# The first expert's w1 scaled quarter by quarter, buffers of their own for the first two attention blocks, and another order of early loads

## The chip, the cores and the metric

One core of one Trainium2 chip runs the whole kernel as one program. The metric is the device time of one execution in microseconds (us), taken as the median of several runs.

## The reference

Chunked attention comes first. For 4 batches and 8 heads of 64, each chunk of 32 queries sees 56 keys (16 to the left, its own 32, 8 to the right) and 8 memory keys. Its output `x` (3072 tokens by 512) goes into a mixture of 8 experts whose weights `P` come from a gate through 8 rounds of row and column normalising:

```
a = softmax(scale * q_c @ [mem_k, k_ctx].T);  x_c = a @ [mem_v, v_ctx]
logits = x @ w_gate;  P = exp(logits - max)
8 times: P /= P.sum(1) ; P /= P.sum(0) ; P *= N / E
for e in range(8):  out += P[:, e:e+1] * (relu(x @ w1[e]) @ w2[e])
```

All of it is float32. w1[e] is 512 by 1024, w2[e] is 1024 by 512.

## The kernel before

**Products.** TensorE multiplies in float16. Each float32 operand is scaled by a power of two and split into a high and a low float16 part, and three products (`PASSES`) stand for one. `split` (L508) does this: ScalarE writes the high part (L513), VectorE the low part (L521). The scale is found first: `most` (L555, its instruction at L558) reduces the absolute maximum per partition, and `scales` (L434) brings the partitions together by a transposition on TensorE (`turned_max`, L488, at L494), a reduction of one row (L502), a rounding to a power of two (L450, L451), a product with ones that spreads the value (L481) and a reciprocal (L456, L457). From the second expert on, the products follow a seven-product block scheme (`hidden`, `output`, with `product` at L1598).

**Tiles.** Tokens come in 6 units of 512 (`NU`), a unit in 4 attention blocks of 128 tokens and in two halves `g` of 256. A unit's work for one expert is 4 quarters `fp` of the 1024 hidden features. A w1 quarter is 512 by 256 floats, loaded by `load` (L536) in two transfers with rows of 128 floats (L549); a w2 quarter is one transfer (L551). The first unit of the first expert is done plainly: `first_hidden` (tile `pp`, L2045) makes 2 feature halves times 2 k halves times 6 matmuls of 256 columns for each quarter and half, and `plain_output` (tile `yp`, L2126) 6 matmuls of 512 columns for each quarter and block of tokens.

**Attention block n.** `load_block` (L848 for q, L842 to L845 for k), `load_extra` (rows `kx` that neighbour the block and the memory keys, L782 to L790) and `load_values` (v in windows, one transfer for each chunk and parity, L921; memory values L890) fetch it. Then: transpositions `tq` (L1006) and `tk` (L1010), copies into `qT` and `kC` (L1014 to L1034, ScalarE), scores `sp` (L1069), maximum and difference (L1083, L1089, VectorE), exp (L1108), transposition `ta` (L1127), values `xp` (L1137), division (L1155 to L1157), transposition `xt` (L1178), copy into `xg` (L1184). `qT` and `kC` exist once, so block 1 waits for block 0's scores. The first half's scale of x comes from the maxima of v of blocks 0 and 1 (L974).

**Order.** Nothing is scheduled by the compiler: each step is a task with an engine, a modelled cost, a priority and its predecessors. `Plan.run` (L164) takes for each engine the task that can start first, ties by priority, and writes the instructions in that order; each engine then runs its list strictly in order. Transfers are tasks of SP (some of ScalarE) with a modelled share `dma` of the transfer engines. Where TensorE would be idle over 0.4 us in the attention stage, `pad` (L126) fills in matmuls on the identity matrix whose result nobody reads (tile `warm`, L427). `BLOCKS`, `VALUES` and `FIRST` (L732 to L734) hold the priorities of the early loads; the lowest is first. Here w1's four quarters come behind q, k and v of blocks 0 and 1.

**First expert's weights.** `fetch_first` loads four quarters, finds four maxima and one scale over all (`scale_w`), and only then `plain1` (w1) or `plain2` (w2) may split any quarter.

## Time and profile before

| | us |
|---|---|
| median of 3 runs | 1921.87 |
| lowest, highest | 1920.07, 1922.44 |
| the profiled execution's own time | 1919.81 |
| its span, first to last instruction | 1917.9 |

The page gives busy time for each engine; TensorE's includes the `warm` matmuls, and its granted clock is 1.00 over the span. A row of instructions gives its start, its length, engine, line, operation, the tile written and read, and how often it stands there in a row (x); what is in square brackets is the engine's idle time before it and what ended it. The suffix q (SPq) means the issuing queue of that engine.

### The profile page before, as it was taken

Reading aid. Unit: us, or ns where it says so; the run is one execution under the profiler, and the core shown is the slowest. Engines: PE = TensorE matmul, PEld = TensorE weight load, DVE = VectorE, ACT = ScalarE, POOL = GpSimd, SP = SyncE. Lnnn points to the kernel's source line nnn. Section 1 sums busy time; section 2 is a strip of 40 time slices with the busy share of each in tenths; the row PEclk is TensorE's granted clock in tenths of the full one; section 3 lists DMA queues with packets and bytes.
Section 4 is the critical chain, followed back from the end, with each engine's and each line's share of the span. In section 5 each row is a group of like instructions: output and inputs, shape, how many; then the busy total and the mean of one; then the engine's idle time right before and its main releaser. Section 6 shows DMA issues by size and latency. Waiting matters only on the chain.

```text
span 1917.9 us, 47295 instructions
## 1 busy us (share of the span) xinstructions
PE 1903.2 (99%) x19616; PEld 1641.0 (86%) x19616; DVE 1436.4 (75%) x2396; ACT 1033.6 (54%) x2019; POOL 524.4 (27%) x549
## 2 busy tenths in 40 slices
PE   9999999999999999999999999999999999999999
PEld 7777676688888888888888888888888888888888
DVE  6776569778679866898668875898678885786565
ACT  4765565556456545646445554655555554564453
POOL 1220001544224221432124231342124232332112
PEclk9999999999999999999999999999999999999999
DMA  8678753453235342265214533245313732322321
GB/s 198 174 194 209 171 172 116 129 204 125 83 110 172 127 148 85 78 197 185 92 63 149 197 105 127 78 160 176 138 45 105 242 122 94 100 83 84 127 83 67
DMA packets 246791, 254.82 MB, mean 133 GB/s; under 512 B 113264, under 2 KB 180272, under 8 KB 242224
## 3 DMA queue, kind: packets, MB, share of 16 engines
q1 hardware_dynamic: 244452, 251.21, 41.2%
q8 instruction: 153, 2.51, 0.6%
q10 hardware_dynamic: 2124, 0.59, 0.2%
q14 instruction: 62, 0.51, 0.1%
HBM read 187.84 MB, written 63.44 MB: 131 GB/s over the span
## 4 chain that ended last, share of the span: by engine, by line
PE 96%; DMA 2%; DVE 1%; ACT 0%; issue 0%; SPq 0%; ACTq 0%; DVEq 0%
PE px L1598 26%; PE yx L1598 23%; PE pz L1598 13%; PE yz L1598 11%; PE py L1598 6%; PE yp L2126 6%; PE yy L1598 6%; DMA q<-in_q_dram 1%; PE xp L1137 1%; PE sp L1069 1%; PE pp L2045 1%; PE tq L1006 1%; PE tk L1010 0%; PE ta L1127 0%; PE xt L1178 0%; DVE w L521 0%
## 5 line engine op out<-in xcount | busy, mean ns | idle before, releaser
L1598 PEld LDWEIGHTS <-w 128*128 128x128 f16 x7896 | 771.4, 98 | 91.9 <-issue 0.6
L1598 PEld LDWEIGHTS <-h 128*128 128x128 f16 x7056 | 690.4, 98 | 81.4 <-issue 1.5
L1598 PE MATMUL px<-x,w 128*128 128x256 f16 x4512 | 549.1, 273 | 0.0
L1931 POOL TENSOR_TENSOR acc<-acc,y 128x256 f32<-128x256 f32 x252 | 267.5, 1068 | 862.1 <-ACT y L1906 842.7
L1598 PE MATMUL yx<-w,h 128*128 128x256 f16 x4032 | 467.5, 273 | 1.3 <-DVE acc L1941 1.3
L1657 ACT ACTIVATE q<-px 128x256 f32<-128x256 f32 x376 | 142.8, 381 | 294.2 <-PE px L1598 289.5
L1598 PE MATMUL pz<-x,w 128*128 128x256 f16 x2256 | 278.2, 273 | 0.0
L1598 PE MATMUL yz<-w,h 128*128 128x256 f16 x2016 | 233.8, 273 | 0.0
L1826 DVE TENSOR_TENSOR h<-ss,h 128x1024 f16<-128x1024 f32 x160 | 215.0, 1346 | 4.0 <-ACT h L1802 3.5
L1777 ACT ACTIVATE h<-c 128x768 f16<-128x768 f32 x168 | 140.8, 838 | 106.4 <-DVE c L1667 106.4
L1802 ACT CAST h<-ss 128x1024 f16<-128x1024 f32 x168 | 174.1, 1039 | 20.4 <-DVE ss L1766 19.6
L1766 DVE SCALAR_TENSOR_TENSOR ss<-c,ss 128x256 f32<-128x256 f32 x336 | 168.3, 501 | 8.2
L1810 DVE SCALAR_TENSOR_TENSOR h<-c,h 128x768 f16<-128x768 f32 x168 | 165.3, 984 | 9.2 <-ACT h L1777 9.1
L1667 DVE SCALAR_TENSOR_TENSOR c<-px,q 128x256 f32<-128x256 f32 x188 | 78.0, 422 | 103.2 <-PE px L1598 94.9
L1906 ACT ACTIVATE y<-yx,pscale 128x256 f32<-128x256 f32 x168 | 79.4, 473 | 114.8 <-PE yx L1598 110.6
L1598 PE MATMUL py<-x,w 128*128 128x256 f16 x1128 | 139.2, 273 | 0.0
L2126 PE MATMUL yp<-w,h 128*128 128x512 f16 x576 | 132.0, 379 | 0.0
L1667 DVE SCALAR_TENSOR_TENSOR c<-py,q 128x256 f32<-128x256 f32 x188 | 78.5, 422 | 60.2 <-PE py L1598 56.7
L1766 DVE SCALAR_TENSOR_TENSOR ss<-c,h 128x512 f32<-128x512 f32 x168 | 120.8, 719 | 3.1 <-ACT h L1754 3.0
L1598 PE MATMUL yy<-w,h 128*128 128x256 f16 x1008 | 116.9, 273 | 0.0
L2126 PEld LDWEIGHTS <-h 128*128 128x128 f16 x576 | 56.0, 98 | 57.9
L513 ACT ACTIVATE w<-ws,sw 128x1024 f16<-128x1024 f32 (+1 forms) x64 | 69.3, 1089 | 65.5 <-POOL ws L602 65.5
(158 smaller groups left out, 1773.0 us busy)
## 6 DMA issues: line engine op xcount, KB each, us to landing
x<-xkeep SPq DMA_DIRECT2D x28, 1792.0 KB
akeep<-acc SPq DMA_DIRECT2D x168, 256.0 KB
acc<-akeep SPq DMA_DIRECT2D x168, 256.0 KB
w1f<-in_moe_w_dram SPq DMA_DIRECT2D x72, 256.0 KB
w2f<-in_moe_w_dram SPq DMA_DIRECT2D x32, 512.0 KB
w1fm<-in_moe_w_dram SPq DMA_DIRECT2D x56, 256.0 KB
w2fm<-in_moe_w_dram SPq DMA_DIRECT2D x28, 512.0 KB
xkeep<-x SPq DMA_DIRECT2D x6, 1792.0 KB
```

The costliest lines, as they stand in the source:

```text
L513: lambda: nc.scalar.activation(dst(0), src(), AF.Copy, scale=s),
L1598: nc.tensor.matmul(dst.t, a, b, start=(not more and n == 0), stop=(n == end), skip_group_check=more,)
L1657: lambda: nc.scalar.activation(t.t, src.t, AF.Copy, scale=DOWN),
L1667: lambda: nc.vector.scalar_tensor_tensor(c.t[:, o], src.t, DOWN, q.t, op0=ALU.mult, op1=ALU.add),
L1766: lambda: nc.vector.scalar_tensor_tensor(dst(), src(), 0.0, other(), op0=ALU.max, op1=op),
L1777: lambda: nc.scalar.activation(h.t[:, 0, 0:3], c.t, AF.Relu),
L1802: lambda: nc.scalar.copy(h.t[:, 0, 3:7], ss.t),
L1810: lambda: nc.vector.scalar_tensor_tensor(h.t[:, 1, 0:3].rearrange("p a n -> p (a n)"), c.t.rearrange("p a n -> p (a n)"), 0.0, h.t[:, 0, 0 ...
L1826: lambda: spare.tensor_tensor(h.t[:, 1, 3:7], ss.t, h.t[:, 0, 3:7], op=ALU.subtract),
L1906: (lambda: nc.scalar.activation(t.t, src.t, AF.Copy, scale=f))
L1931: lambda: nc.gpsimd.tensor_tensor(acc.t[:, cols], acc.t[:, cols], q.t, op=ALU.add),
L2126: nc.tensor.matmul(py.t, hf.t[:, hl, where[fh], o : o + P], room(fp, WIDE * wl + DM * fh, WIDE * wl + DM * (fh + 1)), start=(fp == 0 and i ...
```

## The change

1. Each w1 quarter of expert 0 has a scale of its own. `total` replaces `most`: a sum of absolute values per partition, on ScalarE with an accumulating output for five of the eight quarters (`SUMS`), on VectorE for three. `scale_first` adds over the partitions by one product with ones and makes the scale with four small VectorE operations. w2's quarters keep a common scale, multiplied for each quarter by the inverse of w1's.
2. Blocks 0 and 1 have `qT`, `kC` and the transposed weights `aT` apart (lent from tiles that are idle yet), take `kx` straight from PSUM, and their larger copy into `kC` is on VectorE.
3. Memory values of batch 0 are loaded once and spread by GpSimd; all v loads of blocks 0 and 1 move to SP's queue and wait for that; the `kx` loads of blocks 0 and 1 move to ScalarE's queue. Three high parts of the first expert's splits (one w1, two w2) move to GpSimd.
4. A w1 quarter is 256 neighbouring columns: one transfer with rows of 256 floats, for all experts. w2's rows are grouped to match.
5. An exp on one column right at the start takes the load of ScalarE's table. Early loads with a priority below -10 start strictly in turn, over all queues. The planner's model of transfers is another one, with smaller costs; `PACE` goes from 38.0 to 38.4.

```
-ISSUE = 0.5
+ISSUE = 0.45
+LANES = 8
...
+        turns = sorted((t for t in self.tasks if t.dma and t.prio < IN_TURN), key=lambda t: t.prio)
+        for a, b in zip(turns, turns[1:]):
+            a.behind = [b]
+            b.left += 1
...
-                at = max(at, dma - BEHIND)
-                t.start = at
-                clock[t.eng] = at + t.cost
-                dma = max(dma, at + t.cost / 2) + t.dma
-                t.end = max(dma, at + t.cost) + 2.6
+                if self.fill is None:
+                    at = max(at, dma - BEHIND)
+                t.start = max(at, lanes[0])
+                for _ in range(t.count):
+                    at = max(at, lanes.pop(0))
+                    work = t.dma / t.count
+                    if self.fill is None:
+                        work *= SHARE
+                    dma = max(dma, at + BEGIN) + work
+                    lanes.append(dma + AFTER)
+                    at += ISSUE
+                clock[t.eng] = at
+                t.end = dma + AFTER
...
+    first = misc.tile([P, 1], F32, name="first")
+    nc.scalar.activation(first, one, AF.Exp)
...
-    PACE = 38.0
+    PACE = 38.4
...
+    def scale_first(fp, t, prio):
+        c = slice(fp, fp + 1)
+        whole = bank("att", [P, 1], f"whole_{fp}")
...
+            lambda: nc.tensor.matmul(whole.t, ones, mxs[:, 0, 0, c], start=True, stop=True),
...
+            nc.vector.tensor_scalar_max(u, whole.t, 2.0**-100)
+            nc.vector.tensor_scalar(
+                u.bitcast(I32), u.bitcast(I32), 0x7F800000, None, op0=ALU.bitwise_and
+            )
+            nc.vector.tensor_scalar_mul(u, u, 2.0**-14)
+            nc.vector.reciprocal(sf[:, 0, c], u)
...
+        def spared():
+            nc.gpsimd.tensor_scalar(dst(0), src(), s, None, op0=ALU.mult)
...
-    w1v = w1.rearrange("e (kt p) (fh fp f) -> e fp p kt fh f", p=P, fh=2, fp=FP)
-    w2v = w2.rearrange("e (fh fp p) d -> e fp p fh d", fh=2, fp=FP)
+    w1v = w1.rearrange("e (kt p) (fp f) -> e fp p kt f", p=P, fp=FP)
+    w2v = w2.rearrange("e (fp fh p) d -> e fp p fh d", fh=2, fp=FP)
...
-                for fh in range(2):
-                    queue.dma_start(st.t[:, fh], w1v[e, fp, :, :, fh])
+                queue.dma_start(st.t.rearrange("p k a f -> p k (a f)"), w1v[e, fp])
...
+            nc.scalar.activation(room(0, 0, 1024), st.t.rearrange(flat), AF.Abs, accum_out=dst)
...
-            sw[:, 0, 0:1],
-            [known[0, 1], ld],
+            sf[:, 0, fp : fp + 1],
+            [known[0, 1, fp], ld],
...
-    BLOCKS = (-50.0, -44.0, -30.0, -26.0)
-    VALUES = (-47.0, -41.0, -28.0, -24.0)
-    FIRST = (-38.0, -20.0)
+    BLOCKS = (-57.56, -49.14, -31.37, -14.83)
+    SUMS = ("AAAD", "ADAD")
+    KX_AT = -47.74
+    VALUES = (-45.76, -42.53, -25.94, -11.5)
+    FIRST = ((-46.33, -38.4, -19.16, -28.68), (-18.82, -23.03, -25.93, -18.46))
...
+                lv = [spread_out[n]]
             lv = lv + [
-                add(eng, parts, lambda i=i, on=on: go_v((i,), on), lv, at, [vt], dma=1.35)
-                for i, (eng, on) in enumerate(
-                    (("SP", nc.sync), ("ACT", nc.scalar) if n < 2 else ("SP", nc.sync))
-                )
+                add("SP", parts, lambda i=i: go_v((i,), nc.sync), lv, at + i, [vt], dma=VWORK)
+                for i in range(2)
             ]
...
-        kC = rings["kC"].take(lambda k: kC_tile)
+        if n == 1:
+            lent = operands("h", [P, 2, 7, GT], "early_operands", 3)
...
+            kC = rings["kC"].take(lambda k: piece(0, c=CB), 1)
+            qT = rings["qT"].take(lambda k: piece(HP * CB * KW), 1)
...
+        eng, copy = ("DVE", nc.vector.tensor_copy) if n < 2 else ("ACT", nc.scalar.copy)
...
-                dma=7.0,
+                dma=4.3,
...
+    t = add("ACT", 2, memory_rows, (), -49.4, dma=0.1)
+    spread_out.append(add("POOL", 0.9, lambda: spread(nc.gpsimd, 0), [t], -48.0))
+    spread_out.append(add("POOL", 1.1, lambda: spread(nc.gpsimd, 1), [t], -47.0))
```

## Rows read from the trace of the kernel before

**Rows 1.** The page: busy time of the engines over the span.

```profile
PE 1903.2 (99%) x19616; PEld 1641.0 (86%) x19616; DVE 1436.4 (75%) x2396; ACT 1033.6 (54%) x2019; POOL 524.4 (27%) x549
```

**Rows 2.** Busy time by stage: stretch, length, PE, PEld, DVE, ACT, POOL, PEclk, DMA share, GB/s.

```profile
0.00:34.00 34.00, 30.04 (x470) 24.40 (x471) 17.36 (x36) 14.71 (x26) 4.95 (x12) 1.00 0.82 182
34.00:66.00 32.00, 30.88 (x602) 23.38 (x602) 28.67 (x47) 24.07 (x46) 5.33 (x5) 1.00 0.74 173
66.00:120.00 54.00, 51.83 (x958) 38.90 (x959) 37.07 (x68) 37.51 (x77) 16.21 (x21) 1.00 0.77 207
120.00:290.00 170.00, 167.07 (x2982) 122.69 (x2960) 107.01 (x210) 96.19 (x198) 11.58 (x16) 1.00 0.69 181
```

**Rows 3.** The same view for line L427 (`warm`) alone: stretch, length, PE, PEld, PEclk.

```profile
0.00:34.00 34.00, 20.71 (x157) 15.83 (x157) 1.00 0.82 182
34.00:66.00 32.00, 0.49 (x3) 0.29 (x3) 1.00 0.74 173
```

**Rows 4.** Timeline from the last maximum of w1 to the first `pp` matmul.

```profile
26.36 1.21 DVE L558 TENSOR_REDUCE mxs<-w1f 128x1 f32<-128x1024 f32 x1
...
28.04 0.13 DVE L445 TENSOR_REDUCE most_of<-mxs 128x1 f32<-128x4 f32 x1
...
29.09 1.33 ACT L513 ACTIVATE x<-xg,sx 128x512 f16<-128x512 f32 x2 [0.42 <-DVE sx L457]
...
29.84 0.75 DVE L521 SCALAR_TENSOR_TENSOR x<-xg,sx,x 128x512 f16<-128x512 f32 x1 [0.32 <-ACT x L513]
...
30.70 0.16 DVE L457 RECIPROCAL sw<-uw 128x1 f32<-128x1 f32 x1
...
33.38 1.14 PE L2045 MATMUL pp<-x,w 128*128 128x256 f16 x6
```

**Rows 5.** Timeline of SP's queue, the early issues.

```profile
0.73 0.45 SPq L848 DMA_DIRECT2D q<-in_q_dram  x1
1.23 0.57 SPq L842 DMA_DIRECT2D k<-in_k_dram  x1
...
15.94 5.81 SPq L549 DMA_DIRECT2D w1f<-in_moe_w_dram  x8
...
24.08 5.50 SPq L921 DMA_DIRECT2D w<-in_v_dram  x8
...
30.79 4.06 SPq L921 DMA_DIRECT2D w<-in_v_dram  x8
```

**Rows 6.** Groups by line: VectorE and ScalarE to 66 us, GpSimd to 110 us.

```profile
L521 DVE SCALAR_TENSOR_TENSOR w<-w1f,sw,w 128x1024 f16<-128x1024 f32 x4 | 4.9, 1278 | 0.0
L558 DVE TENSOR_REDUCE mxs<-w1f 128x1 f32<-128x1024 f32 x4 | 4.8, 1212 | 0.0
...
L513 ACT ACTIVATE w<-w1f,sw 128x1024 f16<-128x1024 f32 x4 | 4.4, 1143 | 0.0
...
L1034 ACT ACT_TABLE_LOAD x1 | 1.3, 1283 | 9.1 <-DMA v_pair<-in_v_dram 9.1
...
L602 POOL TENSOR_TENSOR ws<-w1f 128x256 f32<-128x256 f32 x7 | 5.1, 726 | 33.4 <-DMA w1f<-in_moe_w_dram 16.8 <-DMA v_pair<-in_v_dram 7.3 <-ACT x L513 5.5
L602 POOL TENSOR_TENSOR ws<-ws,w1f 128x256 f32<-128x256 f32 x4 | 4.1, 1028 | 0.3
...
L913 POOL COPY w<-v_pair 128x1040 f32<-128x1040 f32 x2 | 2.1, 1050 | 11.5 <-DMA v_pair<-in_v_dram 11.5
```

**Rows 7.** The chain that ended last: its first DMA piece, and one run of 24 matmuls.

```profile
1.84 4.79 DMA k<-in_k_dram
...
402.74 2.62 PE yy L1598 x24
```

**Rows 8.** Timeline: the first `yp` matmuls.

```profile
55.87 1.46 PE L2126 MATMUL yp<-w,h 128*128 128x512 f16 x6
```

**Rows 9.** Waits of TensorE for data from 34 to 300 us: total, times, longest.

```profile
PE tq L1006 <- DMA q<-in_q_dram: 2.4, 3, 1.1
```

**Rows 10.** One five-us stretch, columns as in the view of rows 2.

```profile
20.00:25.00 5.00, 4.55 (x98) 3.63 (x96) 4.97 (x7) 1.80 (x3) 0.00 (x0) 1.00 1.08 302
```

More of the change, by code (lines that the diff above doesn't have):

```diff
@@ L23 @@
 HSHIFT = 18
-ISSUE = 0.5
+HFIRST = 12
+ISSUE = 0.45
+LANES = 8
+VWORK = 1.1
+WORK2 = 1.8
+BEFORE = 0.7
+TABLE = 0.9
+COLD = 4.5
 BEHIND = 5.0
-FIRST = 2.0
+SHARE = 1.5
+BEGIN = 1.0
+AFTER = 1.2
+LATER = 1.0
 MARGIN = 8.0
@@ L29 @@
 FAR = 60.0
+IN_TURN = -10.0
 class Task:
-    __slots__ = ("eng", "cost", "fn", "prio", "left", "ready", "end", "then", "takes", "frees", "n", "dma", "start", "many")
+    __slots__ = ("eng", "cost", "fn", "prio", "left", "ready", "end", "then", "takes", "frees", "n", "dma", "start", "many", "count", "behind")
 class Past:
@@ L110, in add @@
         t.many = many
+        t.behind = ()
+        t.count = cost
         if dma:
@@ L217, in run @@
                     heappush(self.free[b.group], (b.end, b.bank))
+            for s in t.behind:
+                s.left -= 1
+                s.ready = max(s.ready, t.start)
+                if s.left == 0:
+                    heappush(waiting[s.eng], (s.ready, s.n, s))
             lag = 0.0 if t.dma else 0.2 if t.eng == "PE" else 0.12
@@ L384, in tile_chunked_attn_sinkhorn_moe @@
     ring("at", range(1))
+    ring("aT", range(2))
     ring("g", range(3))
@@ L431, in tile_chunked_attn_sinkhorn_moe, with scales @@
     counted = [0]
-    def scales(part, s, u, name, deps, prio, pool=None):
+    def scales(part, s, u, name, deps, prio, pool=None, shift=SHIFT):
         n = s.shape[-1]
@@ L824, in load_extra @@
             return
-        t1 = part(slice(0, 2 * KR), loads[0:2], at, tx, tx)
+        t0, t1 = [
+            add(
+                "PE",
+                0.35,
+                lambda n=n: turn(slice(n * KR, (n + 1) * KR)),
+                loads[n : n + 1],
+                at + n,
+                [kx],
+                takes=None if n else tx,
+            )
+            for n in range(2)
+        ]
         t2 = part(slice(2 * KR, P), loads[2:4], needed(1) - 2.0, tx, None)
-        extra[u] = (kxT, [t1, t1, t2, t2])
+        extra[u] = (kxT, [t0, t1, t2, t2])
+        straight.append(tx)
+    straight = []
+    more = []
     def flat(t, i, r=slice(0, P)):
@@ L938, in load_values @@
             fill_ones = add("POOL", 0.3, lambda: nc.gpsimd.memset(vt.t[:, :, :, D:DV], 1.0), (), at, [vt])
-        parts = CB + (first or last)
+        parts = CB + (n == EARLY - 1)
         if n < BU:
@@ L1618, in hidden @@
         nm = f"{e}_{u}_{fp}"
+        down = DOWN if e > 0 else DOWN0
         (w, wmade), (x, xmade) = wo[e, fp, 1], xops[u]
@@ L1656, in read @@
                 0.4,
-                lambda: nc.scalar.activation(t.t, src.t, AF.Copy, scale=DOWN),
+                lambda: nc.scalar.activation(t.t, src.t, AF.Copy, scale=down),
                 [dep],
@@ L1706, in hidden @@
                 0.4,
-                lambda: nc.scalar.activation(c.t[:, 3], px.t, AF.Copy, scale=DOWN),
+                lambda: nc.scalar.activation(c.t[:, 3], px.t, AF.Copy, scale=down),
                 [t4],
@@ L1744, in hidden @@
             0.4,
-            lambda: nc.scalar.activation(rr(1), px.t, AF.Relu, scale=DOWN),
+            lambda: nc.scalar.activation(rr(1), px.t, AF.Relu, scale=down),
             [t4],
@@ L2171, in fetch_first @@
         for fp in range(FP):
-            st, ld = load(0, fp, which, FIRST[which - 1] + 0.5 * fp)
-            staged.append((st, ld))
-            found.append(most(0, fp, which, st, [ld], at - 12.0))
-        scale_w(0, which, found, at - 10.0, "att")
+            st, ld = load(
+                0, fp, which, FIRST[which - 1][fp], after=spread_out[:1] if which == 1 and fp else ()
+            )
+            if which == 1:
+                o = operands("w1", [P, 2, 7, 2, P], f"w1_0_{fp}")
+                staged.append((st, ld, o))
+            else:
+                staged.append((st, ld))
@@ new lines, in fetch_first, with together @@
+            found.append(total(0, fp, which, st, [ld], at - 12.0 + ((17.68, 19.5, 24.87, 5.01), (3.31, -26.43, 9.29, -16.2))[which - 1][fp]))
+            if which == 1:
+                found[-1].ready = SINCE[fp]
+            if which == 1:
+                c = slice(fp, fp + 1)
+                known[0, 1, fp] = scale_first(fp, found[-1], at - 10.0 + fp)
+        if which == 1:
+            known[0, 1] = known[0, 1, FP - 1]
+            return staged
+        def together():
+            nc.vector.tensor_tensor(mxs[:, 0, 1], mxs[:, 0, 1], uf, op=ALU.mult)
@@ L2232, in turn @@
                     plan.free[group] = []
-            att_tasks = lgs + [xkept[v] for v in range(KEEP)] + list(gkept.values())
+            att_tasks = lgs + [xkept[v] for v in range(KEEP)] + list(gkept.values()) + list(sxs.values())
             opened[0] = add("-", 0.0, turn, att_tasks, -2000.0)
```

278 lines of the change are left out of this document (181 added, 97 removed).

## The prediction

> **What bounds the kernel now.** I read the page first: TensorE is busy 1903.2 of 1917.9 us [rows 1], so only what makes TensorE idle, or busy with nothing, can cost or save time. The view by stages tells where that is [rows 2]: TensorE's idle time is the length less its busy time, 3.96 us before 34 us, 1.12 from there to 66, 2.17 to 120, 2.93 to 290. Then the same view for the `warm` filler alone [rows 3]: 20.71 us before 34 us and 0.49 to 66. So up to 34 us TensorE does 30.04 - 20.71 = 9.3 us of work that counts, and 24.7 us are waste; behind that the stages to 290 us lose 6.2 us of idle time and hardly any filler. The start is what can be won. All DMA, VectorE and ScalarE times matter only as far as they move the first `pp` matmul, at 33.38 [rows 4], or leave TensorE without work later.
>
> Read back from 33.38, two legs end together [rows 4]. The x leg: the first half's x is split from 29.09 on (its first low part starts at 29.84). The w1 leg: the last of four maxima ends at 27.57, the reduction over partitions starts at 28.04, the scale is there at 30.86, 2.8 us later, and only then a first quarter is split. Both lie behind one queue: SP issues w1's eight transfers from 15.94 to 21.75 [rows 5].
>
> **The w1 leg after the change.** Needed for the first `pp` is one quarter, 512 KB, in place of 2 MB. It stands seventh or so in turn, in front of v. At 302 GB/s, the rate of the stretch in which w1 comes [rows 10], 512 KB take 1.7 us. q, k of two blocks and kx are some 1.2 MB before it; at 200 GB/s (an estimate below that rate, since their rows are shorter) 6 us from about 2 us on. So it is there by about 11. Then a sum, 1.2 us on ScalarE: no such row, bounds 1.14 (an activation of the same size) and 1.14 + 1.28 (a table load, if Abs were to need one) [rows 6]; I take 1.2. One product and four small operations with their hand-overs: the old reduction had seven and took 2.8 [rows 4]; 1.5 for the new one. A split 1.14 + 1.28 [rows 6]. The quarter is ready at about 17; it no longer decides.
>
> **The x leg after the change.** It ends with block 1's v. SP issues first: four transfers for q and k, 0.45 to 0.57 each [rows 5], 2.0; two for kx, 1.1; one for w1, 5.81 / 8 = 0.73. That ends at 0.73 + 3.8 = 4.5. The v transfers now wait for the memory values, which ScalarE issues behind its table load of 1.28 [rows 6] and kx, so at about 3.5. Their landing has no row: a k transfer took 4.79 from its issue, with the first loads around it [rows 7], the upper end; no row excludes next to nothing for 16 KB, the lower; half of 4.79, 2.4, taken. Then GpSimd spreads them, 1.05 by its copy of 1040 columns [rows 6]: v starts at about 7.0. Sixteen issues follow on SP, at 4.06 / 8 = 0.51 to 5.50 / 8 = 0.69 each [rows 5]; at 0.55, nearer to the end with less in the queue, they end at 15.8. ScalarE's queue no longer shares this. Landing 2.4 again, maximum 1.2, scale 2.8 as for w1, split of x 0.67 + 0.75 [rows 4, 6]: **23.6 for the first `pp`**. The ends: 17.5, where the w1 leg takes over, if both landings take next to nothing and an issue 0.45; 30.6 if both take 4.8 and an issue 0.69. Block 1's own chain from v to `xg` (values, division, transposition, copy, some 3.8 us) runs beside the scale and ends earlier. That block 1 has buffers of its own takes its transpositions and scores out of block 0's way, and the larger copy of its keys off ScalarE; behind v's landing both are hidden, so I give them nothing. With v at its lower end the chain of 3.8 would be the next to decide, as long as the maximum and the scale together. ScalarE's queue gets five issues of kx and memory values ahead of its first copy; at 0.57 at most they end near 4.8, when the first k lands [rows 5, 7], and if they ended 1 us later block 0 alone would be later, which waits for v anyway.
>
> **What the start is worth.** Before the first `pp` TensorE did 9.3 less the 0.6 of `pp` before 34, 8.7 us, some of it for block 2, which will come later: 7.4 remain. Waste until the first `pp`: before 33.4 - 8.7 = 24.7, after 23.6 - 7.4 = 16.2. **Gain 8.5**, ends 14.6 and 1.5.
>
> **What is given back.** From 23.6 on TensorE needs work. There are 96 `pp` matmuls of the first half (4 quarters of 24), 2.62 / 24 = 0.109 each [rows 7], 10.5 us, and block 2, 3.7 us as half of the 7.4: 14 us. The outputs `yp`, at 55.87 before [rows 8], need all of w2. Behind v stand three quarters of w1, four of w2, q, k and v of block 2: 4.5 MB, 15 us at 302 GB/s, so about 33; a sum, a scale over all (2.8), a split: about 41. 17.4 us to fill with 14.2: 3.2 us of waste, where the old stage to 66 us lost 1.12 + 0.49 [rows 2, 3]. **Given back 2**, rounded up; ends 0, if block 3 comes in time to fill, and 6, if w2 comes 4 us later. VectorE is the other limit: 17.36 + 28.67 = 46 us of work up to 66 us [rows 2], of which five sums of 1.21 go to ScalarE [rows 6] and about 4 us come (two copies, four scales): 44 us, from 7 us on, so the whole of w2 is split at about 53 at the earliest; `yp` takes it quarter by quarter.
>
> Three high parts go from ScalarE to GpSimd. Its copy of about that size took 1.05; its additions with two inputs 0.73 for 256 columns, and 1.03 in another group of the same form [rows 6]. Ends 1.05 and four times 1.03; both hidden by the other quarters' `pp`, so nothing in the sum. The Trainium skill, GPSIMD Engine Reference, section Key points, speaks against this move: GpSimd shares its SBUF interfaces with VectorE and contends with VectorE instructions that read two SBUF inputs. VectorE's low parts are of that kind; the 0.73 and 1.03 would fit that, but no row proves it. By it each of the three would wait for a low part of 1.28, and the sum would be up to 1.3 us worse.
>
> **Later.** One w1 transfer for two saves SP issues beyond the start, the splits read w1 with a stride, and `PACE` moves by 0.4: TensorE does not wait there for weights, so nothing for all three; without that cover the issues would be 0.73 each. The new model of transfers reorders all of the stage to 290 us, whose 6.2 us of idle time [rows 2] could fall or grow: 0, ends -3 and +3. Behind it nothing changes but the start. Sum: 8.5 - 2 = 6.5. The profiled 1919.81 becomes 1913.3; it stands 2.06 under the median, so **1915.4** against 1921.87.
>
> **Rivals.** *Nothing to do* (0.17): loads of w1 and w2 come as late as the upper ends, TensorE waits between `pp` and `yp` what it waited before it. For it: 6 us given back, and 302 GB/s is a full rate already, with a DMA share of 1.08 [rows 10]. Against it: bytes moved before 34 us were only 182 GB/s on average [rows 2]. Gain 8.5 - 6 = 2.5, down to 0: 1919.4 to 1922. In the same case falls that a scale for each quarter does not do what it says because splits queue on VectorE in another order. *More* (0.13): the x leg near its lower end, later idle time falls too: gain 12 to 15, 1907 to 1910. *Slower* (0.12): attention of the blocks behind the start. The old model counted 7.0 for a store of x where the new one counts 4.3, and 1.55 for q where it is now 1.25, so loads are planned closer to their use, and TensorE, in order, stands at `tq` when q is late. It did so three times, 2.4 us in total, 1.1 at most [rows 9]. Twenty blocks come behind the first four. From 10 such waits of 1.1 the gain of 6.5 is gone and 3.8 us are lost beside, about 1926. Against it: only three of the blocks waited so far, and the new order loads earlier.
>
> **How the numbers follow.** The forecast has 0.58: its own range is 1911 to 1919. 0.2% of 1921.87 is 3.8 us, about what a measurement can tell from no change; faster is below 1918.0. Forecast 0.54 below it, and *more* 0.13, with 0.05 of *nothing to do* if little is given back: 0.72. Same: 0.04 and 0.12 of these, 0.16. Slower 0.12. The range takes the forecast, most of *nothing to do* and half of *more*: 1907 to 1922.
>
> **What would show it.** Right: first `pp` at 20 to 28 us; `warm` before 34 us at 8 to 14 in place of 20.7; SP's v issues from 7 to 17 without pause; `yp` from 40 to 46; waits at `tq` up to 300 us under 4 us in total. Wrong: a first `pp` behind 30, or TensorE idle or in `warm` for over 6 us between it and `yp`, or a total of waits at `tq` over 8.

## The result and the profile after

| | before | after |
|---|---|---|
| median, us (21 runs each, taken together) | 1920.89 | 1923.85 |
| the profiled execution's own time | 1919.81 | 1925.82 |
| its span | 1917.9 | 1923.9 |

The ratio is 1.0015, 95% interval 1.0009 to 1.0022: slower by 3 us, clear of the noise but inside the 0.2% that was named as no change, outside the range of 1907 to 1922, and on the other side of the forecast of 1915.4. The profiled execution of after is the second longest of its 21 and stands 1.97 above its median, that of before 1.08 below its own, so the spans differ by 6.0 where the medians differ by 2.96.

The page of after answers to [rows 1]: TensorE has 101 matmuls fewer, all fillers and more (58 `warm` in place of 168), and still a longer span.

```profile
PE 1898.3 (99%) x19515; PEld 1634.6 (85%) x19515; DVE 1436.9 (75%) x2407; ACT 1035.3 (54%) x2025; POOL 546.7 (28%) x555
```

The stages, as in [rows 2], with three finer stretches:

```profile
0.00:34.00 34.00, 27.85 (x483) 22.47 (x483) 20.04 (x46) 17.54 (x36) 11.09 (x16) 0.95 0.89 209
34.00:66.00 32.00, 28.97 (x574) 20.75 (x575) 26.86 (x52) 23.53 (x45) 11.73 (x7) 1.00 0.67 142
66.00:120.00 54.00, 45.14 (x797) 32.74 (x796) 33.51 (x58) 32.11 (x66) 17.04 (x21) 0.94 0.82 214
120.00:290.00 170.00, 168.47 (x3016) 125.91 (x3018) 108.72 (x209) 98.94 (x207) 12.37 (x16) 1.00 0.66 171
...
85.00:90.00 5.00, 0.48 (x3) 0.49 (x4) 1.71 (x2) 2.08 (x5) 1.43 (x3) 0.76 0.99 243
90.00:95.00 5.00, 5.00 (x85) 4.17 (x85) 1.06 (x3) 2.13 (x4) 1.39 (x3) 0.56 0.78 192
95.00:100.00 5.00, 5.00 (x93) 3.30 (x92) 2.57 (x6) 3.74 (x9) 0.00 (x0) 1.00 0.85 232
```

The same view for `warm` alone, as in [rows 3]:

```profile
0.00:34.00 34.00, 8.92 (x54) 5.96 (x54) 0.95 0.89 209
34.00:66.00 32.00, 0.60 (x4) 0.39 (x4) 1.00 0.67 142
```

These two views give a sum. Waste (idle time and `warm`) before 34 us is 34 - 27.85 + 8.92 = 15.07 in place of 24.67: 9.6 less. A mean granted clock of 0.95 over 34 us takes about 1.7 of that back (an estimate: 5% of the length). From 34 to 66 it is 3.63 in place of 1.61: 2.0 given back. So up to 66 us the change wins 5.9; 6.5 was forecast. Then comes the loss: from 66 to 120 us TensorE is idle for 8.86 in place of 2.17, and the clock of 0.94 costs 3.2 more: 9.9 lost. The stage to 290 wins 1.4. By this sum the change is 2.6 behind at 290 us.

The sum is too kind to the change, as a mark in both kernels shows: the first `yx` (the second expert's first output product) starts 5.0 later (before first, then after).

```profile
399.96 2.24 PE L1598 MATMUL yx<-w,h 128*128 128x256 f16 x19
405.00 2.24 PE L1743 MATMUL yx<-w,h 128*128 128x256 f16 x19
```

What the sum misses, 2.4 us, stays open; possibly TensorE counts as busy also where its matmuls stand loosely, and the 9.6 is too high; no run shows it. From there to the end some 1.2 more go (below).

Most of the loss has one place in this execution. TensorE's timeline of after and its waits from 34 to 300 us, against [rows 9]:

```profile
82.00 0.82 PE L2191 MATMUL pp<-w,w 128*128 128x256 f16 x6
89.52 0.90 PE L1135 MATMUL tq<-ident,q 128*128 128x128 f32 x3 [6.70 <-DMA q<-in_q_dram]
```

```profile
PE tq L1135 <- DMA q<-in_q_dram: 7.3, 2, 6.7
```

And SP's queue in front of it (after first, then before, with TensorE's two rows):

```profile
77.64 0.45 SPq L1401 DMA_DIRECT2D xkeep<-x  x1
78.18 0.39 SPq L622 DMA_DIRECT2D w1f<-in_moe_w_dram  x1
78.66 1.58 SPq L970 DMA_DIRECT2D q<-in_q_dram  x1
```

```profile
78.32 0.60 SPq L1256 DMA_DIRECT2D xkeep<-x  x1
79.01 0.45 SPq L848 DMA_DIRECT2D q<-in_q_dram  x1
...
87.14 0.86 PE L1137 MATMUL xp<-x_room,at 64*32 64x65 f32 x64
89.10 0.66 PE L1006 MATMUL tq<-ident,q 128*128 128x128 f32 x4 [1.10 <-DMA q<-in_q_dram]
```

The q of block 8 stands behind the first store of x (1792 KB) in both kernels and lands some 10 us after its issue in both: 78.66 to 89.5, and 79.01 to 89.1. Before, TensorE had `pp` and `xp` until 88, so only 1.1 us of it showed; that is the 1.1 of [rows 9]. After, TensorE's list has `tq` next at 82.8. Behind the wait the granted clock is 0.56 for five us, most of it at 1.2 GHz. The kernel's own plan says why: with the store at 4.3 it has q landing at 75.8 and `tq` at 77.4, while SP issues q 12.7 us later than planned (78.66 against 66.0). The plan of the kernel before, with the old model of transfers, has it landing at 88.3, close to what was measured (89.1).

Of the start, SP's queue (as in [rows 5]), the engines around the first `pp` (as in [rows 4]), the high parts on GpSimd (as in [rows 6]), and the first `yp` (as in [rows 8]):

```profile
7.04 0.39 SPq L622 DMA_DIRECT2D w1f<-in_moe_w_dram  x1
8.51 7.85 SPq L1038 DMA_DIRECT2D v_pair<-in_v_dram  x16
```

```profile
12.89 1.05 ACT L646 ACTIVATE w<-w1f 128x1024 f16<-128x1024 f32 x1
13.85 0.19 ACT L646 ACTIVATION_READ_ACCUMULATOR w<-w1f 128x1 f32 x1
...
19.36 1.22 DVE L1086 TENSOR_REDUCE vmax<-v_pair 128x1 f32<-128x1024 f32 x1 [1.80 <-DMA v_pair<-in_v_dram]
20.61 0.15 DVE L492 TENSOR_REDUCE most_of<-vmax 128x1 f32<-128x2 f32 x1
20.68 1.28 DVE L595 SCALAR_TENSOR_TENSOR w<-w1f,sf,w 128x1024 f16<-128x1024 f32 x1
...
22.84 0.69 DVE L1302 TENSOR_TENSOR xq<-xp,rec 128x512 f32<-128x512 f32 x1
...
23.63 0.16 DVE L504 RECIPROCAL sx<-ux 128x1 f32<-128x1 f32 x1
24.95 0.59 ACT L1329 COPY xg<-xt 128x512 f32<-128x512 f32 x1 [0.26 <-PE xt L1323]
25.57 1.34 ACT L587 ACTIVATE x<-xg,sx 128x512 f16<-128x512 f32 x2
25.83 1.20 DVE L649 TENSOR_REDUCE mxs<-w1f 128x1 f32<-128x1024 f32 x1
26.94 1.41 DVE L595 SCALAR_TENSOR_TENSOR x<-xg,sx,x 128x512 f16<-128x512 f32 x2
27.17 0.35 PE L542 MATMUL whole<-mxs,one 128*128 128x1 f32 x2
27.39 1.06 PE L2191 MATMUL pp<-x,w 128*128 128x256 f16 x6
```

```profile
L582 POOL TENSOR_SCALAR w<-w2f,sf 128x1024 f16<-128x1024 f32 x2 | 6.0, 2986 | 18.1 <-DVE most_of L492 11.3 <-PE xp L1282 6.8
...
L582 POOL TENSOR_SCALAR w<-w1f,sf 128x1024 f16<-128x1024 f32 x1 | 3.8, 3827 | 10.4 <-DMA w<-in_v_dram 10.4
```

```profile
47.84 1.46 PE L2272 MATMUL yp<-w,h 128*128 128x512 f16 x6
```

The first `pp` comes at 27.39 (before 33.38, forecast 23.6), the first `yp` at 47.84 (before 55.87, forecast 41).

### The profile page after: what moved, and what is told of

It is laid out like the page before. It is cut to its first block, busy times and chain, and to the rows that moved or that the text cites. A ratio compares the mean times of both kernels' runs of the same rounds, so it can differ in the third digit from the quotient of the medians.

```text
span 1923.9 us, 46983 instructions
## 1 busy us (share of the span) xinstructions
PE 1898.3 (99%) x19515; PEld 1634.6 (85%) x19515; DVE 1436.9 (75%) x2407; ACT 1035.3 (54%) x2025; POOL 546.7 (28%) x555
## 4 chain that ended last, share of the span: by engine, by line
PE 91%; DVE 4%; DMA 2%; SPq 1%; issue 1%; ACT 1%; POOL 0%; ACTq 0%; DVEq 0%; POOLq 0%
PE px L1743 24%; PE yx L1743 23%; PE pz L1743 12%; PE yz L1743 11%; PE py L1743 6%; PE yy L1743 6%; PE yp L2272 5%; PE xp L1282 1%; DMA q<-in_q_dram 1%; DVE ss L1912 1%; PE sp L1199 1%; DVE h L1956 1%; PE pp L2191 1%; PE xt L1323 1%; DVE x L595 1%
## 5 line engine op out<-in xcount | busy, mean ns | idle before, releaser
L2077 POOL TENSOR_TENSOR acc<-acc,y 128x256 f32<-128x256 f32 x252 | 276.9, 1106 | 865.5 <-ACT y L2052 852.3
L1972 DVE TENSOR_TENSOR h<-ss,h 128x1024 f16<-128x1024 f32 x160 | 207.0, 1296 | 3.7 <-ACT h L1948 3.7
L1948 ACT CAST h<-ss 128x1024 f16<-128x1024 f32 x168 | 174.2, 1040 | 25.2 <-DVE ss L1912 24.9
L1912 DVE SCALAR_TENSOR_TENSOR ss<-c,ss 128x256 f32<-128x256 f32 x336 | 172.7, 514 | 8.2
L1956 DVE SCALAR_TENSOR_TENSOR h<-c,h 128x768 f16<-128x768 f32 x168 | 166.1, 989 | 10.7 <-ACT h L1923 10.5
L1813 DVE SCALAR_TENSOR_TENSOR c<-pz,q 128x256 f32<-128x256 f32 x188 | 78.7, 422 | 26.7 <-PE pz L1743 25.4
```

The source lines that it names most:

```text
L1813: lambda: nc.vector.scalar_tensor_tensor(c.t[:, o], src.t, down, q.t, op0=ALU.mult, op1=ALU.add),
L1912: lambda: nc.vector.scalar_tensor_tensor(dst(), src(), 0.0, other(), op0=ALU.max, op1=op),
L1948: lambda: nc.scalar.copy(h.t[:, 0, 3:7], ss.t),
L1956: lambda: nc.vector.scalar_tensor_tensor(h.t[:, 1, 0:3].rearrange("p a n -> p (a n)"), c.t.rearrange("p a n -> p (a n)"), 0.0, h.t[:, 0, 0 ...
L1972: lambda: spare.tensor_tensor(h.t[:, 1, 3:7], ss.t, h.t[:, 0, 3:7], op=ALU.subtract),
L2077: lambda: nc.gpsimd.tensor_tensor(acc.t[:, cols], acc.t[:, cols], q.t, op=ALU.add),
```

## The experiments

Eighteen kernels. An interval reaches about 0.001 to either side of its ratio, 2 us, so the profiles, one execution of each kernel, carry much of the argument. "First pp" and "first yx" are the starts of these matmuls; "waits" are TensorE's at `tq`, `tk` and `tx` for q, k and kx from 34 to 300 us, total. Before has 33.4, 2.4 and 400.0.

| run | built on | first pp | waits | first yx | ratio to before, interval |
|---|---|---|---|---|---|
| after | | 27.4 | 7.5 | 405.0 | 1.0015 (1.0009 to 1.0022) |
| e1_store7 | after | 27.6 | 3.1 | 395.6 | 0.9992 (0.9983 to 1.0001) |
| e3_before_store43 | before | 33.7 | 3.9 | 402.5 | 1.0006 (0.9997 to 1.0015) |
| e4_q_first | after | 28.6 | 3.9 | 398.4 | 1.0008 (0.9999 to 1.0017) |
| e16_q_ahead | after | 27.6 | 6.0 | 402.8 | 1.0012 (1.0004 to 1.0020) |
| e11_store_act | after | 27.7 | 10.5 | 408.9 | 1.0058 (1.0045 to 1.0070) |
| e2_no_pool | after | 27.0 | 4.1 | 402.4 | 1.0022 (1.0013 to 1.0031) |
| e5_one_scale | e1 | 33.7 | 2.3 | 403.7 | 1.0026 (1.0017 to 1.0035) |
| e6_shared | e1 | 26.9 | 0.7 | 402.0 | 1.0008 (0.9999 to 1.0018) |
| e8_x_first | e1 | 27.6 | 0.0 | 396.9 | 1.0004 (0.9995 to 1.0013) |
| e9_two_swaps | e1 | 28.1 | 5.5 | 398.3 | 1.0002 (0.9993 to 1.0011) |
| e7_old_late | e1 | 26.0 | 4.9 | 396.8 | 1.0016 (1.0007 to 1.0025) |
| e10_old_late_costs | e1 | 27.0 | 3.6 | 395.1 | 0.9985 (0.9976 to 0.9994) |
| e12_swaps_late | e9, e10 | 28.5 | 4.7 | 397.7 | 0.9987 (0.9979 to 0.9996) |
| e13_pp_free | e10 | 26.4 | 3.8 | 398.9 | 0.9990 (0.9981 to 0.9998) |
| e15_keep10 | e10 | 25.9 | 1.1 | 391.6 | 0.9962 (0.9950 to 0.9974) |
| e14_pp_free_keep10 | e13, e15 | 27.0 | 0.6 | 393.9 | 0.9967 (0.9954 to 0.9979) |
| e17_after_store10 | after | 27.4 | 1.3 | 395.1 | 0.9988 (0.9978 to 0.9997) |
| e18_before_store10 | before | 33.6 | 0.8 | 397.5 | 1.0005 (0.9996 to 1.0013) |

The waits alone don't order the times: e6 and e8 have next to none and are no faster than e1. Their changed starts give other orders later, with idle time elsewhere.

### What gives the start's gain back: the store of x

e1 puts the old cost of the store back into the changed kernel; e3 puts the new one into the kernel before.

```
 def keep(at, done):
...
-    dma=4.3,
+    dma=7.0,      # e1; e3: 7.0 to 4.3 in before
```

> Changed kernel, with the planner's cost of the stores of x put back from 4.3 to 7.0 and nothing else. Theory 'the start was won and given back at one q': in the changed kernel TensorE stands 6.7 us at tq of block 8, whose q is queued behind the 1.8 MB store of unit 0's x. With 7.0 the plan puts that tq 2.2 us later with other work ahead of it, so the wait falls to about 4.5 us and the time by 2 to 3 us, to about 1921. Rival 'later reordering all over': the wait only turns up elsewhere and the time stays within 1 us of 1923.9.

> Kernel before with one number of the change: the planner's cost of the stores of x at 4.3 in place of 7.0. The plan puts tq of block 8 2.9 us earlier there. Theory 'one q': its wait grows from 1.1 to about 4 us and the time by 2 to 3 us over the kernel before (to about 1923.5). Rival 'reordering all over': no single wait grows by more than 1 us; the time is within 1 us of the kernel before.

e1: no wait at this `tq` is left, the waits for q are 1.0 in all, and the time is 0.23% below after, 4.4 us, more than the 2 to 3 expected. What is left is one wait of 2.1 at `tk`, for a k that stands behind the second store of x. e3: the long wait appears in the kernel before as well (3.6), with a granted clock of 0.75 from 90 to 100 us; the time, 0.06% above, is not told from no change. So 4.3 in place of 7.0 makes this wait longer in either kernel, and costs time in the changed one.

How it does so, the two orders tell. Up to TensorE's `pp` at 82 us every engine's order is the same in after, e1, e10, e15 and e17, and SP's up to 98 us: q stands behind the store in all five. What the number moves is the work ahead of `tq`; in e1 it starts here:

```profile
74.05 1.61 SPq L970 DMA_DIRECT2D q<-in_q_dram  x1
...
85.12 0.60 PE L1135 MATMUL tq<-ident,q 128*128 128x128 f32 x4
```

That is 2.3 us more work than after has in front of it (82.8). SP also issues q 4.6 us earlier than in after (78.66), and this can't be the number's doing: SP's list is the same there, and so are all others up to then. With SP at e1's pace q would land at about 84.9 in after, and the wait be about 2 (an estimate: 74.05 and the 10.9 us of after). So a good part of the 6.7 belongs to this one execution; the medians, 4.4 us apart, are the measure of the number.

e4 lets the store wait in the plan until q and k of block 8 have landed; e16 only writes it behind them in SP's order (`hold`: the instruction is written behind the one named, the plan stays).

```
+        if n == 8:                      # e4
+            for t in (lq, lk):
+                t.then.append(xkept[0])
+                xkept[0].left += 1
+        if n == 8:                      # e16: written behind lk, planned as before
+            plan.hold[xkept[0]] = lk
```

> Changed kernel in which the store of unit 0's x waits until q and k of block 8 have landed; nothing else. Theory 'one q': the wait at tq of block 8 falls from 6.7 us to under 1, TensorE keeps its full clock there, and the time falls by 7 to 9 us, to 1915 to 1917. Rival 'the store takes its toll anyway': the store now stands before q of blocks 9 and 10, TensorE waits there, and the gain is under 3 us.

> The changed kernel (store costed 4.3) with one swap in SP's order: the first store of x is issued behind q and k of block 8 instead of just ahead of them, all else in its place. Theory: q stood behind 1.8 MB; in front of it, it lands 2.5 to 5 us after its issue, TensorE's wait at tq falls from 6.7 to under 1.5, the half clock behind it goes, the first px comes at 104 to 107 instead of 112.4, and the time is 5 to 8 us below the changed kernel (ratio to before 0.9975 to 0.999). Rival: q is late for its issue, not for the store (SP gets to it 12 us after its planned time); then it lands within 3 us of before, the wait stays above 4 and the ratio above 1.0005.

Both miss what was expected of the time (0.07% and 0.03% below after, inside the noise). In both q is nearly in time, and the wait goes to the next load in the queue, kx:

```profile
84.79 0.66 PE L1148 MATMUL tk<-ident,k 128*128 128x128 f32 x4
90.30 1.11 PE L920 MATMUL tx<-ident,kx 128*128 128x128 f32 x4 [4.85 <-DMA kx<-in_k_dram]
```

That is e16, where `tq` now runs at 83.42 and kx stands behind the store. In e4 it doesn't: TensorE waits 3.0 for kx until 83.40, and the store leaves only at 87.53. So the theory was right on q and wrong on the price: the store is not the only thing that makes a load late there. The plan wants block 8 sooner than SP's queue brings it.

e11 takes the stores to another queue.

```
-    lambda: nc.sync.dma_start(xkeep[u], ...),
+    lambda: nc.scalar.dma_start(xkeep[u], ...),
```

> The changed kernel (store costed 4.3, so q of block 8 right behind it in the order), with the stores of x issued on ScalarE's queue instead of SP's. Theory: the small load is late because it stands behind 1.8 MB in the same queue; on another queue q lands 3 to 5 us after its issue, TensorE's wait at tq falls from 6.7 to under 2, first px from 112.4 to 104 to 107, time 4 to 6 us below the changed kernel (ratio to before 0.998 to 0.9995). Rival: it is the transfer engines that are full, whatever the queue; then q lands 7 us or more after its issue, the wait stays over 4, and the ratio stays at 1.0015.

The worst of all, a miss for both the theory and its rival. The store leaves at 69.0, and SP's queue stands still (eight issues of v in 11.31 us; after: 4.96). The view of SP's waits names what for:

```profile
67.43 11.31 SPq L1038 DMA_DIRECT2D v_pair<-in_v_dram  x8
...
82.33 0.46 SPq L970 DMA_DIRECT2D q<-in_q_dram  x1
```

```profile
SPq L1038 <- DMA xkeep<-x: 7.9, 1, 7.9
```

The fourth load of v waits until the store has landed, because in the trace both use the same semaphore (103): the wait was written into the program by the move. So e11 doesn't show what the store's bytes cost another queue. Nor does q's shorter landing, 5.7 us after its issue (at 88.04) in place of 10.9: it is issued 3.7 later than in after, when the store is over.

e17 and e18 set the store to 10.0, near the time from q's issue to its landing behind it in the trace, in the changed kernel and in the kernel before.

> The changed kernel with one number other: the planner's cost of a store of x is 10.0 instead of 4.3 (with 7.0 the ratio to before was 0.9992, with 4.3 it is 1.0015). Theory: that number alone gave the start's gain back; with it near the store's real time the waits of TensorE for q and k to 300 us fall below 2 in total, the first px comes at 101 to 104, and the time is 1914 to 1916 (ratio 0.997 to 0.998), 2 us of it still lost in the five waits behind 600 us. Rival: the old late planning took part in the gain of the run with 10.0 in another way than by those 2 us; then the ratio is 0.9985 or above.

> The kernel before with the store of x costed 10.0 instead of 7.0: it tells whether the gain of the runs with 10.0 belongs to the change's earlier start or to that number by itself. Theory: before had only 2.4 us of waits for q in all, of which this can take 1 to 2: ratio 0.999 to 1.0005. Rival: the number alone is worth 4 us or more also without the change: ratio below 0.998.

With 10.0 the waits fall to 1.3, and the changed kernel is 0.27% faster than with 4.3, but not the 0.35 to 0.45% that the theory gave; the ratio is where the rival had it. At the first `yx` e17 is 9.9 us ahead of after and 4.9 ahead of before; behind it the lead goes. From 290 to 460 us TensorE is idle for 2.9 (170 less 167.06), one wait of 2.2 for ScalarE's `y` among it, and the granted clock is 0.66 from 410 to 415. The kernel before is not faster with 10.0 (1.0005), and its trace looks alike: 2.5 ahead of before at the first `yx`, then 4.2 idle from 290 to 460 us, with a wait of 2.1 for `y`. So up to the first `yx` the number is worth 9.9 in the changed kernel and 2.5 in the kernel before (one execution each): most of what it costs is tied to the change, whose earlier start takes cover away. Why 10.0 brings the wait for `y` stays open; e15 below has 10.0 and the old planning there, and no such wait.

### The late loss

In the changed kernel TensorE stands five times behind 460 us, once for an expert from 624 us on, 0.23 each and 1.2 in all; before has no such row.

```profile
PE px L1743 <- DVE c L1813: 1.2, 5, 0.2
```

VectorE's timeline in front of the first of them (after), with TensorE's row behind it:

```profile
616.98 1.21 DVE L631 TENSOR_REDUCE mxs<-w2fm 128x1 f32<-128x1024 f32 x1
618.11 1.27 DVE L595 SCALAR_TENSOR_TENSOR w<-ws,sw,w 128x1024 f16<-128x1024 f32 x1
619.30 0.42 DVE L1813 SCALAR_TENSOR_TENSOR c<-py,q 128x256 f32<-128x256 f32 x1
...
624.78 1.47 PE L1743 MATMUL px<-x,w 128*128 128x256 f16 x12 [0.23 <-DVE c L1813]
```

A maximum and a split of the next weights (2.5 us) stand in a place where VectorE seems to have no slack. e7 takes the old model of transfers from the end of the attention stage on, with the new costs; e10 takes the old costs there too, which gives the order of the kernel before.

```
+if t.dma and self.fill is None:          # e10
+    many = 2 if t.dma == 1.5 else t.count        # e7: t.count
+    share = {1.5: 2.1, 1.8: 2.1, 4.3: 7.0, 0.7: 1.3}.get(t.dma, t.dma)
+    at = max(at, dma - BEHIND)
...
+    dma = max(dma, at + many * 0.25) + share     # e7: t.dma
+    t.end = max(dma, at + many * 0.5) + 2.6      # e7: and LATER
...
```

> The changed kernel with the store of x costed 7.0 again, in which the planner uses the old model of transfers from the end of the attention stage on (about 280 us); up to there nothing differs. Theory: the five waits of TensorE for VectorE, 0.4 us each, once for an expert from 600 us on, come from the order in which the new model lets the weights' maxima and splits fall on VectorE; they go, and the time falls by 2 us against the kernel with the store at 7.0 alone (ratio to before 0.998). Rival: they come from w1's new layout (splits that read with a stride, other transfers), which stays here; then the five waits stand and the time is the same (0.999).

> The changed kernel with the store of x costed 7.0 again, in which behind the attention stage the planner uses the old model of transfers with the old costs of w1, w2, x and the sums too (the run before this kept the new costs). The kernel's own order there is then that of the kernel before. Theory: the five waits of 0.4 us, once for an expert from 600 us on, come from that order; they go, and no others come: 2 us below the kernel with the store at 7.0 alone, ratio to before about 0.998. Rival: they come from w1's new layout in SBUF and its transfers, which stay: five waits of 0.4, ratio 0.999.

e7: the five waits go and others come (1.8 for ScalarE's `q`, 1.5 in three for `c`); a miss, and slower. e10: no row of TensorE waiting behind 460 us; its ratio is 0.07% below e1's, which the intervals don't tell from none. The layout of w1 is the same in both, so the waits come from the order, not from the layout.

e15 takes the store at 10.0 in place of 7.0 in e10.

> The kernel with the old planning behind the attention stage and the store costed 10.0 instead of 7.0, the start as the change has it. Theory: waits of TensorE for q and k from 66 to 300 us under 1.5 in total (with 4.3: 7.3; with 7.0: 3 to 4), time 1 to 3 us below the kernel with 7.0. Rival: 7.0 was enough, what is left of these waits has another cause, and 10.0 changes nothing or makes it worse: ratio 0.9985 or above.

```profile
0.00:34.00 34.00, 26.35 (x483) 20.88 (x483) 19.85 (x46) 18.27 (x37) 11.07 (x16) 1.00 0.89 220
34.00:66.00 32.00, 30.02 (x577) 21.04 (x578) 27.31 (x53) 23.26 (x46) 11.72 (x7) 1.00 0.68 141
66.00:120.00 54.00, 52.92 (x1011) 41.10 (x1010) 38.04 (x71) 39.41 (x82) 15.03 (x21) 1.00 0.83 225
120.00:290.00 170.00, 168.73 (x2861) 121.60 (x2859) 107.59 (x215) 96.91 (x201) 15.58 (x21) 1.00 0.64 173
```

This beats both kernels: 1912.78 against 1920.13, 7.3 us, and e10 by 0.23%, with intervals apart. Idle time to 120 us behind 66 is 1.08, the clock stands at 1.00 in all four, and the waste before 34 us is 7.65 and 8.79 of `warm`, 16.4: 8.2 less than before.

### The start

e2 puts the three high parts back on ScalarE (`spare=False`).

> Changed kernel with the three high parts of splits back from GpSimd on ScalarE. GpSimd took 3.83, 3.13 and 2.85 us for them where the planner has 1.3 and ScalarE takes 1.15. Rival 'GpSimd holds up the start': the last w1 and w2 quarters are ready 2 to 3 us sooner, TensorE's waits between the first pp and 70 us fall by 2 us and the time falls by 2 us or more. Theory 'one q': the start may be 1 us better, the wait at tq of block 8 stays at 6 to 8 us and takes it back; the time stays within 1 us of 1923.9.

No gain: the first `pp` stands at 27.0, the ratio at the edge of after's interval. GpSimd's 2.9 to 3.8 us are hidden. One thing was expected otherwise: the wait at `tq` of block 8, expected to stay at 6 to 8, is 1.7 (SP issues q at 74.46 here), with 1.4 at `tx` behind it, and yet the time is no better. The long wait of the profiled after is thus one form of the loss; here it came as several, with 4.1 idle and a granted clock of 0.94 from 66 to 120 us.

e5 lets every quarter's scale wait for all four sums, and loads the four quarters in a row behind v of block 1 so that these come early; e6 gives block 1 the `qT` and `kC` of block 0 (`aT` stays apart).

```
-    FIRST = ((-46.33, -38.4, -19.16, -28.68), ...       # e5
+    FIRST = ((-41.4, -41.3, -41.2, -41.1), ...
...
-                known[0, 1, fp] = scale_first(fp, found[-1], ...)
+            for fp in range(FP):         # e5, behind the loop
+                known[0, 1, fp] = scale_first(fp, found, ...)
...
-        if n == 1:                       # e6
+        if False:
             lent = operands("h", [P, 2, 7, GT], "early_operands", 3)
```

> The changed kernel with the store of x costed 7.0 again, in which each quarter's scale waits for the sums of all four quarters; to let these come early, the four quarters are loaded one behind the other, right behind v of block 1. It undoes what the scale for each quarter is for. Theory: the scale for each quarter is what lets the first pp start before most of w1 is there. SP ends v at about 16, four issues of 0.7 follow, 2 MB at 200 to 300 GB/s land at 25 to 28, then a sum 1.2, a scale 2, a split 1.2: first pp at 30 to 32 in place of 27.6, time 3 to 5 us above the kernel with the store at 7.0 alone (ratio to before 1.0008 to 1.002). Rival: w1 does not decide at all, the x leg alone does; then the first pp stays within 1 us of 27.6.

> The changed kernel with the store of x costed 7.0 again, in which block 1 takes block 0's qT and kC (it waits for block 0's scores again); aT stays apart. Theory: v's landing at 18.4 decides for block 1, so its transpositions and scores may end 1 to 3 us later and cost nothing: first pp at 27 to 28.5. Rival: the buffers of block 1 are what brought the first pp forward; then it comes at 30 or later. The order that the kernel plans for itself behind 34 us differs too (about 5 us more idle TensorE in its plan), so the total may be up to 5 us worse in either case and is not what tells them apart.

e5 brings the first `pp` back to 33.7, where it was before, with v there as early as ever (maximum of block 1's v at 18.8). So the scale for each quarter, with the loads that it allows, is what brings the first `pp` forward. About 2 of the 6.1 us are e5's own (an estimate): it still makes four scales, and VectorE does them in a row, from 29.48 to 32.09, before the first low part. e6: 26.9, close to the 27 to 28.5 expected; a `qT` and `kC` of its own for block 1 bring the first `pp` nothing.

What then holds the first `pp` at 27.4? In the timeline above it comes 0.2 us after `whole`, the product for a w1 quarter that it doesn't need, whose sum stands ahead of x's low part on VectorE. e8 moves w1's low split (20.68) behind block 1's division; e9 also the sum and its product behind x's low parts; e13 the product, and the scale and GpSimd's part that need it, behind the third `pp` group. e9 and e13 change the order alone (`hold`), e8 the plan.

```
+    plan.hold[wo[0, 0, 1][1][0]] = t        # e9, e13: low split, until the division
...
+    plan.hold[sum3[0]] = done[-1]           # e9, e13: sum, until x's low parts
+    plan.hold[wholes[-1]] = done[-1]        # e9: product, the same
...
+    for later_ in (wholes[-1], known[0, 1, FP - 1], spares[0]):   # e13: until pp 3
+        plan.hold[later_] = t
```

> The changed kernel with the store of x costed 7.0 again, in which the low part of w1's first split waits for block 1's division, so that on VectorE the division comes ahead of it. Theory: behind v's landing the first pp hangs on VectorE's order, and the low split (1.28) stood in block 1's chain: first pp at 26.0 to 26.6 in place of 27.6. Rival: the scale of x, not block 1's chain, ends last as the prediction had it; then the first pp stays at 27.4 or later, since the low split now stands behind. The later order changes too (about 4 us more idle TensorE in the kernel's own plan), so the total may rise by that in either case.

> The changed kernel with the store of x costed 7.0 again, and with two instructions of VectorE issued later, all else in the kernel's own order: the low part of w1's first split behind block 1's division, and the sum of w1's last quarter (with its product with ones on TensorE) behind the low parts of the first half of x. Theory: the first pp hangs on VectorE's fixed order, in which the sum of a quarter that the first pp doesn't need, and that waits for its own load, stands ahead of x's low part; moving only the low split did nothing, since that sum then ended last (26.0 to 27.2, behind 1.75 of waiting for w1). First pp at 25.5 to 26.2 in place of 27.6, time 1 to 1.5 us below the kernel with the store at 7.0 alone. Rival: block 1's chain over ScalarE (qT, xg, the high part) ends last; then the first pp stays above 27.

> The kernel with the store at 7.0 and the old planning behind the attention stage, and in the start: the low part of w1's first split behind block 1's division, the sum of w1's last quarter behind x's low parts, and its product with ones on TensorE behind the third pp group instead of ahead of the first. Theory: in all runs so far the first pp began 0.21 us after that product, which it doesn't need; with it moved the first pp comes at 25.0 to 26.2, 1.3 to 2 us earlier than in the runs with this start (27.0 to 28.6 but for one at 26.0), and the time is 1 to 2 us below the kernel with the old late planning alone. Rival: the scale and split of x end no earlier than 27, so the product was only the next in line: first pp above 26.8.

e8 and e9 miss: 27.6 and 28.1, again 0.2 us after `whole`, which in e9 waits 1.77 for the sum. e13 comes at 26.44, just behind the 25.0 to 26.2 expected:

```profile
24.67 0.35 PE L558 MATMUL whole<-mxs,one 128*128 128x1 f32 x2 [0.70 <-ACT xg L1352]
24.88 0.63 PE L1161 MATMUL tk<-ident,k 128*128 128x128 f32 x4
25.35 1.26 PE L488 MATMUL warm<-ident 128*128 128x256 bf16 x10
26.44 0.82 PE L2218 MATMUL pp<-x,w 128*128 128x256 f16 x6
```

v's landing moves by 2 us from run to run, so I count from the start of block 1's v maximum: 6.6 us to the first `pp` in e13 and e14, 7.3 to 9.0 in the runs with the change's order. So the order held it, by some 1.4 us against after's 8.0. But the time is not better (0.9990 against 0.9985, intervals overlapping, where 1 to 2 us less were expected): so small a step of the first `pp` can't be told here. e12 and e14 put the parts together.

> The store of x costed 7.0, the two swaps on VectorE and the old planning behind the attention stage together. Theory: the three add up: ratio to before 0.997 to 0.998, the lowest so far. Rival: what the start wins by the swaps is lost again by 130 us, where k of a later block still stands behind a store of x (2.1 of waiting and 4 us at half the clock before): ratio 0.998 to 0.9992, no better than without the swaps.

> The same with the store of x costed 10.0, about what it takes in the trace from issue to landing (10.8). Theory: with the store's true cost no q or k that TensorE needs soon is put right behind it, so also the wait at tk near 124 us (1.6 to 3.3) and the stretch at half the clock behind it go: 2 to 4 us below the kernel before it, ratio to before 0.996 to 0.998. Rival: the loads are moved earlier and something else is late (w1 of the next expert, v): no better than 0.998.

Neither is below its parent with the change's start (e10, e15): for e12 the rival's ratio came, and e14's 0.9967 lies in the range expected but owes nothing to the swaps.

## Why the prediction was wrong

**What the start is worth** was near the mark by the prediction's own count of waste: 8.5 forecast, 9.6 less 1.7 measured, 8.2 in e15 with a full clock. **Given back 2** was right too (2.0; 1.0 in e15). The sum at 66 us, 6.5, was 5.9.

**"Later: 0, ends -3 and +3"** is the step that failed: 9.9 lost to 120 us and 1.4 won to 290. I took the idle time of the stage as the measure of what could change there. The trace held the other figure: a q 10 us under way, of which 8.9 lay under other work. The new model of transfers plans that q 14 us before it lands (75.8 against 89.5). That the cost of the store in it loses time is shown by e1 and e17, and by e15 against e10; that the rest of the new model does so too is only argued, from e4's wait and from the plans.

**The rival "slower"** named this mechanism (4.3 for 7.0, TensorE standing at `tq`) and had the price wrong: ten waits of 1.1, priced by the wait of before, where it is one wait of 6.7, in the profiled execution, with 3.2 of half clock behind it. Its chance of 0.12 rested on "only three of the blocks waited so far", which counts waits and not how little covered them.

**"Block 1's own chain runs beside the scale and ends earlier"** was wrong: the scale of x is there at 23.79, `xg` at 25.54. Both use VectorE, in one order, with w1's low split between them; behind them a sum and a product for another quarter stand ahead of the first `pp`. Hence 27.4 for 23.6. The v issues (8.51 to 16.36; 7.0 to 15.8 forecast) and v's landing were near the mark. **"It ends with block 1's v"**: it did so no earlier than before (maximum at 19.27 before, 19.36 after). What went was the wait behind four maxima of w1 on VectorE; e5, where the sums of all four decide again, brings the late start back.

**"Behind it nothing changes but the start"**: five waits of 0.23, 1.2 in all, which go with the old model and costs (e10).

Two small sums of the prediction are off and decide nothing: 44 us of VectorE work from 7 us on end at 51, not 53, and ten waits of 1.1 would lose 4.5 us beside the gain, not 3.8.

**The w1 leg at 17** was at 18 for the high part (16.56 to 17.71 on ScalarE) and 22 for the low one, which waits for VectorE. The sum on ScalarE took 1.05 and 0.19 more for reading the accumulator, 1.2 forecast. **GpSimd's parts**, 2.9 to 3.8, lie in the range of 1.05 to 4.1 and are hidden (e2); whether VectorE's low parts slowed them, no run shows. **`yp`** at 47.84 missed 41 by 7: the w2 loads had q, k and v of block 2 among them, and TensorE had work meanwhile.

Not tried: the old model of transfers in the attention stage, with the new start; why SP runs 12 us behind the kernel's plan by 78 us, and why it reaches the store at 72.0 to 77.6 in executions of one order (e15 and after); and why the stretch from 290 to 460 us costs more in some orders (1.4 us idle before, 2.9 in e17).

## What to carry to other kernels

A wait of 1 us can be the tip of a transfer of 10: for every load that a changed order may touch, read issue to landing, not the wait, and then ask what covers the rest. Where a cost model writes the order, its numbers are part of the kernel: with the store at 4.3 the change lost 3 us, with 7.0 it was level with before, and with 10.0, near the time that the trace shows, it won 2, or 7 with the old planning behind the attention stage. One profile is one execution: where two kernels have the same order up to a point, what differs before it is chance, and the medians decide. An instruction just ahead of the critical one in an engine's fixed order is on the critical path, needed or not.

## What was not expected of the hardware

TensorE's granted clock was 0.56 for the five us behind a wait of 6.7 (two levels, 1.2 and 2.4 GHz, so mostly the lower one), and 1.00 in every stage shown of e15, the run without it. Two executions with the same order up to 82 us differ there too: after has 0.95 to 34 us, e1 1.00. SP's queue reached the same store, by the same order, at 72.0 us in one execution and at 77.6 in another. GpSimd takes 2.9 to 3.8 us for a scaling of 128x1024 from f32 to f16 that ScalarE does in 1.15, and 1.05 for a copy of 1040 columns. The Trainium skill, GPSIMD Engine Reference, section 4.1, calls operations with one input roughly line-rate there; the copy, as fast as ScalarE's scaling of 1024, fits that, but the scaling on GpSimd does not, and the measurement decides. Moving a 1.8 MB store to another queue made a load of the first queue wait 7.9 us for the store to land, since both used one semaphore.
